# A linear-attention and state-space kernel whose program is ordered by one wanted time per unit of work, and whose last output leaves by four transfers

## The chip, the cores and the metric

The kernel runs on one core of one Trainium2 chip. The core has five engines that run side by side: TensorE (PE, matrix products, with its weight loads as PEld), VectorE (DVE), ScalarE (ACT), GpSimd (POOL) and SyncE (SP), which here issues every DMA. The metric is the device time of one execution in microseconds. Most executions of one kernel agree within 0.3%.

## The reference

Two independent layers read their own inputs, and their outputs stand side by side in the 1152 columns of each of the 2048 rows. The first is a state-space convolution (S4D), the second a linear attention whose feature map is a softmax and the softmax of the negated values, with 32 heads of 18 columns.

```python
def _A_ref(u, log_A_real, A_imag, C_real, C_imag, log_dt, D_skip):
    dt = jnp.exp(log_dt)
    A = -jnp.exp(log_A_real) + 1j * A_imag
    C = (C_real + 1j * C_imag) * dt[:, None]
    P = jnp.exp((A * dt[:, None])[:, :, None] * pos[None, None, :])
    K = 2.0 * jnp.einsum("dn,dnl->dl", C, P).real
...
    y = jnp.fft.irfft(Uf * Kf[None, :, :], L2)[:, :, :L]
...
    return y + u * D_skip[None, None, :]

def _B_ref(x, wqkv, w_phi, wo):
...
    pq = jnp.einsum("bhsd,hdf->bhsf", q, w_phi)
    pk = jnp.einsum("bhsd,hdf->bhsf", k, w_phi)
    phi_q = jnp.concatenate([_softmax(pq, axis=-1), _softmax(-pq, axis=-1)], axis=-1)
    phi_k = jnp.concatenate([_softmax(pk, axis=-1), _softmax(-pk, axis=-1)], axis=-1)
    kv = jnp.einsum("bhsf,bhsd->bhfd", phi_k, v)
    z  = jnp.einsum("bhsf->bhf", phi_k)
    num = jnp.einsum("bhqf,bhfd->bhqd", phi_q, kv)
    den = jnp.einsum("bhqf,bhf->bhq", phi_q, z)[..., None] + 1e-6
    return (num / den) ... @ wo
...
return jnp.concatenate([a, b], axis=-1)
```

L is 2048, D is 576, and the state has 128 entries for each of the 576 channels.

## The kernel before

The kernel's Python does not write its instructions in the order in which they run. It hands small pieces of work to a planner (class `Plan`): each call of `op` names an engine, an estimated cost, the tiles that it reads and writes, and a function that emits the instructions. `Plan.run` then walks through a made-up clock: at each step it looks, for each engine, at the pieces whose inputs are ready and whose tiles can be had, takes the best by a key, and emits it. The result is one fixed order of instructions for each engine's queue. The chip runs these queues; waits among them are real, and the planner's costs have no further effect. The key is

```python
key = (s if s > at[e] + 100.0 else at[e], ops[k][5], k)
```

Here `s` is the planned start of the piece and `at[e]` the time at which its engine is free. So among pieces that could start within 100 ns of the engine being free, the smaller wanted time (`ops[k][5]`) goes first. The wanted time also sets the order in which pieces take the slots of a tile with few buffers (`place` in `Plan.run`); "pa" and "pb", the PSUM tiles, are free of this order. The wanted time is `pl.now`, set ahead of each unit. Before the change, it grows evenly over the units of one kind:

```python
T_K, D_K = 21.6, 11.6
T_KV = 243.3
T_Q, D_Q = 259.8, 20.2
T_U, D_U = 4.5, 8.6
T_G, D_G = 39.9, 8.0
T_P, D_P, T_P2 = 188.6, 7.7, 393.5
T_Y, D_Y, T_Y2 = 335.1, 8.6, 586.1
```

The attention's units: `fold` multiplies the key weights and later the query weights by the feature map's matrices (tiles wah and wal, one buffer each, so the query weights overwrite the key weights once the last key tile has used them); `whole` loads the value and output weights (wbh, wbl). 16 key tiles (`key_tile`, 128 rows each) load x (tile xi, split into xh and xl), make four groups of 14 matmuls (`gemm`, L326 is the line of every matmul), a softmax (L439 to L449, with the tiles small and e) and a sum over all tiles in PSUM (kvt). `kv` turns that sum into the block matrix kvb. 16 query tiles (`query_tile`) make two such groups of matmuls, a softmax, eleven transposes (L519), the products with kvb, the division, five transposes of the result, two more groups of matmuls, and a store of 128 rows and 576 columns (tile ot, L561).

The convolution's units: 18 units of `u_first` transform the input and store it to DRAM (L587). `mags` and `sel_part` prepare magnitudes, `params` works out phases for 96 channels at a time (six blocks, `par`, for six groups each). 36 groups (`phases`, `waves`, `group`) make the filter for 16 channels each: GpSimd adds phases (PQ), ScalarE takes sines (cs) and exponentials (N), VectorE multiplies them (L747 to L752, into cs and E), and TensorE sums over the state (64 small matmuls reading E and cs). After every ninth group, `k_first` transforms a quarter of the filter and stores it (L772). 2 x 16 `product` units load a block of the input's and the filter's spectrum and of the matrices (ub, kb, cm; L812 to L814), multiply (VectorE L337, then GpSimd), transform back and store (zo, L852). The first half needs two quarters of the filter (groups 0 to 17), the second half the other two. 2 x 8 `last` units load zi (L863, two loads each; the first load needs all 16 products of its half), make 32 matmuls, copy the two PSUM tiles to yo, by VectorE and ScalarE, and store yo by two transfers of 128 partitions (L877). The tile yo has two buffers, zi two, e three, PSUM four of each kind.

`first` is shared by `u_first` and `k_first`: two matmuls, on the upper and lower 64 rows, were two entries of the plan, the second ordered behind the first.

Of the kernel before, what the change touches and what calls it, by code (L numbers as in the profile page):

```python
# [22 lines left out]
W = 4 * DG  # L23
# [108 lines left out]
class Plan:  # L132
# [9 lines left out]
    def __init__(self):  # L142
        self.ops, self.pools, self.free, self.window, self.strict = [], {}, {}, {}, {}
        self.now = 0.0
# [8 lines left out]
    def op(self, eng, cost, fn, r=(), w=(), with_=(), early=0.0, table=None, busy=1.0, lock=False):  # L153
        deps = set()
        for b in r:
            deps.update(b.writers)
        for b in w:
            deps.update(b.readers)
        k = len(self.ops)
        for b in r:  # L160
            b.readers.append(k)
        for b in w:
            b.writers.append(k)
        bufs = list({id(b): b for b in (*r, *w, *with_) if not isinstance(b, Mark)}.values())
        for b in bufs:
            b.left += 1
        self.ops.append([eng, cost, fn, deps, bufs, self.now - early, table, busy, lock and eng])
# [129 lines left out]
PAIR = False  # L297
T_K, D_K = 21.6, 11.6
T_KV = 243.3
T_Q, D_Q = 259.8, 20.2  # L300
T_U, D_U = 4.5, 8.6
T_G, D_G = 39.9, 8.0
T_P, D_P, T_P2 = 188.6, 7.7, 393.5
T_Y, D_Y, T_Y2 = 335.1, 8.6, 586.1


def body(tc, nc, i, out, ctx):
# [27 lines left out]
    def tt(eng, dst, a, b, alu, r, w, n):  # L335
        e = dve if eng == "dve" else pool
        op(eng, c_dve(n) if eng == "dve" else c_pool(n), lambda: e.tensor_tensor(dst(), a(), b(), op=alu), r=r, w=w,  # L337
           lock=eng == "pool" or n > 99 and not any(x.tag in ("pa", "pb") for x in r))
# [8 lines left out]

    ident, ii = B("ident", [128, 128]), B("xl", [128, 128], I32)
# [10 lines left out]
    def fold(w_t):  # L359

        hi, lo, phiw = B("wah", [128, 5, D], F32R), B("wal", [128, 5, D], F32R), B("fT", [128, 5, 126])
        op("sp", 1000, lambda: sp.dma_start(phiw.t, i["wphi"]), w=[phiw])

        def block(g, c, cs):
            wt, pa, pb = B("e", [128, D]), B("pb", [128, 4, 126]), B("pb", [128, 126])
            op("sp", c_dma(c * D * 4), lambda: sp.dma_start(wt.t[:c], w_t[cs, :]), w=[wt])

            def f():
                for k in range(4):
                    mm(pa.t[:, k, :c], wt.t[:c, k * 128:k * 128 + 128], phiw.t[:c, g, :c])  # L370
# [5 lines left out]
            op("pe", 2 * 215, f, r=[wt, phiw], w=[pb], with_=[hi, lo])  # L376
# [33 lines left out]
    def gemm(x, w, ps, o, cs):  # L410

        (xh, xl), (wh, wl) = x, w

        def f():
            p = o()
            for k in range(4):
                mm(p, xh.t[:, k, :], wh.t[:, k, cs], k == 0, False)
                mm(p, xh.t[:, k, :], wl.t[:, k, cs], False, False)
                mm(p, xl.t[:, k, :], wh.t[:, k, cs], False, False)
            mm(p, xh.t[:, 4, :], wh.t[:, 4, cs], False, False)  # L420
            mm(p, xh.t[0:64, 4, :], wl.t[0:64, 4, cs], False, True)
        op("pe", 14 * max(109, (cs.stop - cs.start) / 2.4 + 15), f, r=[xh, xl, wh, wl], w=[ps], busy=0.93)
# [33 lines left out]
    pl.now = 0.0  # L456
    wk = fold(i["wkT"])
    wv = whole(i["wv"])
    kvt = B("pb", [128, 8, 36])
# [27 lines left out]
    pl.now = T_KV  # L487
# [15 lines left out]

    wq = fold(i["wqT"])
    wo = whole(i["wo"])

    def query_tile(t):
        pl.now = T_Q + D_Q * t
# [60 lines left out]
    pl.now = T_U  # L569
# [20 lines left out]
    for c in range(18):  # L590
        pl.now = T_U + D_U * c
# [3 lines left out]
    pl.now = 0.0  # L595
# [7 lines left out]
    def mags():  # L603
# [9 lines left out]
        op("dve", c_dve(n), lambda: dve.scalar_tensor_tensor(C.t, C.t, 1e-30, I.t, op0=ALU.add, op1=ALU.add), r=[C, I], w=[C])  # L613
        op("act", c_act(n), lambda: act.activation(C.t, C.t, AF.Ln), r=[C], w=[C], table="ln")
        op("dve", c_dve(n), lambda: dve.scalar_tensor_tensor(C.t, C.t, 0.5, bc(ldc), op0=ALU.mult, op1=ALU.add), r=[C, ldc], w=[C])
# [11 lines left out]
    pl.now = T_G - 30  # L627
    mags()
    pl.now = 0.0
# [6 lines left out]
    for k in range(3):  # L636
        sel_part(k)
# [6 lines left out]
    def params(blk):  # L644
# [15 lines left out]
        def vs(x, s0, o0, dst, s1=None, o1=None, z=None):  # L660
            k = {} if o1 is None else dict(op1=o1)
            op("dve", c_dve(BW, True), lambda: dve.tensor_scalar(z() if z else dst.t, x.t, s0, s1, op0=o0, **k), r=[x], w=[dst])
# [17 lines left out]
        def flip(full, dst, z=None):  # L680
# [13 lines left out]
        op("dve", c_dve(4 * BW, True), lambda: dve.tensor_scalar(fx.t, p4(), MAGIC, MAGIC, op0=ALU.add, op1=ALU.subtract), r=[pi], w=[fx])  # L694
        tt("dve", p4, p4, lambda: fx.t, ALU.subtract, [pi, fx], [pi], 4 * BW)
        op("dve", c_dve(4 * BW, True), lambda: dve.tensor_scalar(p4().bitcast(I32), p4(), TWO32, BELOW, op0=ALU.mult, op1=ALU.min),
           r=[pi], w=[pi])
# [6 lines left out]
    def phases(g, par):  # L704
        pl.now = T_G + D_G * g
# [7 lines left out]
            x()[:, :, :, 0], pi.t[:, 0:3:2, gs].bitcast(I32).rearrange("p r d -> p d r")), r=[pi], w=[PQ])  # L713
# [8 lines left out]
    def waves(PQ, also):  # L722
# [7 lines left out]
        op("act", 3 * c_act(65 * W) + 250, f, r=[PQ, hp, *also], w=[cs], table="sin")  # L730
        return cs

    def group(g, par, cs, ks):
        pl.now = T_G + D_G * g
# [26 lines left out]
        op("pe", 970, f, r=[E, cs], w=[ps], with_=[ks], busy=0.57)  # L761
# [17 lines left out]
    pl.now = T_G + 20  # L779
# [5 lines left out]
    for g in range(0, NG, 2):  # L785
        blk = g // (NG // NB)
        if par[blk] is None:
            pl.now = T_G + D_G * g - 6
            par[blk] = params(blk), exponents(blk)
        pq = [phases(h, par[blk]) for h in (g, g + 1)]  # L790
        for j, h in enumerate((g, g + 1)):
            pl.now = T_G + D_G * g
# [3 lines left out]
            group(h, par[blk], waves(pq[j], pq[1:] if PAIR and j == 0 else ()), ks)  # L796
            if (h + 1) % (NG // NQ) == 0:
                pl.now = T_G + D_G * h
# [7 lines left out]
    def product(p, half):  # L806

        pl.now = (T_P, T_P2)[half] + D_P * p
# [50 lines left out]
    def last(cb, half):  # L859
        pl.now = (T_Y, T_Y2)[half] + D_Y * cb / 4  # L860
# [11 lines left out]
        op("pe", 520, f, r=[zi, w3], w=ps, with_=[yo], busy=0.4)  # L872
        for r in range(2):
            copy("act" if r else "dve", lambda r=r: yo.t[:, r], lambda r=r: ps[r].t, [ps[r]], [yo], HD)
        for r in range(2):
            st = out.ap[0][0]
            op("sp", c_dma(64 * 2304, 1152), lambda r=r: sp.dma_start(bass.AP(  # L877
                tensor=out.tensor, offset=out.offset + (32 * r + cb) * st + HD * half, ap=[[st, 4], [64 * st, 32], [1, HD]]),
                yo.t[:, r]), r=[yo])
# [26 lines left out]
```

## Time and profile before

| what | before |
|---|---|
| median of 3 runs | 754.59 us |
| lowest, highest | 754.41, 755.47 us |
| the profiled execution's own time | 755.61 us |
| its span, first to last instruction | 753.8 us |
| mean granted TensorE clock | 0.939 |
| bytes moved by DMA | 102.29 MB |

The span is what the trace covers; the time includes what lies around it, 1.8 us here. The clock is a share of full speed. Below, a stage is a stretch of the span between two times, and a row of it gives each engine's busy time in that stretch. The chain of waits is the chain of work that ended last, followed back from the last instruction to what released it.

The 40 slices of the page show the five engines over the span (each digit is the busy share in tenths):

```profile
PE   6799998997997888867999989999979999999965
DVE  2678899877779889687877577786544555555531
ACT  3748787586686877677878576997423335333321
POOL 0475355665555858556857345772103233243100
```

### The profile page before, as it was taken

What the parts mean: (1) busy time and instruction counts of PE and PEld (TensorE: products, weight loads), DVE (VectorE), ACT (ScalarE), POOL (GpSimd) and SP (SyncE); (2) the same over time, 40 slices, a digit from 0 to 9 for tenths busy, and PEclk for the clock granted to TensorE, in tenths of its full rate; (3) what the DMA queues carried; (4) which work ended last, traced back from release to release, by engine and by line L of the source; (5) the groups of instructions that cost most, each with busy time, mean ns of one, the idle gap of its engine ahead of it and who ended that gap; (6) DMA issues with size and microseconds to landing.
All of it is one profiled execution on the core that took longest, in us unless ns stands there. A gap on an engine that the chain in (4) does not pass through costs nothing.

```text
span 753.8 us, 18023 instructions
## 1 busy us (share of the span) xinstructions
PE 670.2 (89%) x7188; PEld 496.6 (66%) x7188; DVE 520.7 (69%) x961; ACT 465.0 (62%) x823; POOL 350.9 (47%) x471
## 2 busy tenths in 40 slices
PE   6799998997997888867999989999979999999965
PEld 4577786874776675645766757766757676768753
DVE  2678899877779889687877577786544555555531
ACT  3748787586686877677878576997423335333321
POOL 0475355665555858556857345772103233243100
PEclk9899999997999987878999999999989999999996
DMA  8943435135441112532455643434577746562653
GB/s 228 334 123 90 129 77 173 53 103 138 103 110 38 50 51 77 122 80 75 139 154 156 175 140 126 156 115 121 133 197 210 234 148 182 154 196 95 180 157 106
DMA packets 114791, 102.29 MB, mean 136 GB/s; under 512 B 43604, under 2 KB 96724, under 8 KB 114708
## 3 DMA queue, kind: packets, MB, share of 16 engines
q1 hardware_dynamic: 114708, 101.15, 47.4%
q8 instruction: 57, 0.93, 0.5%
q14 instruction: 26, 0.21, 0.1%
HBM read 61.98 MB, written 39.06 MB: 134 GB/s over the span
## 4 chain that ended last, share of the span: by engine, by line
PE 47%; DVE 24%; DMA 10%; ACT 8%; issue 2%; POOL 1%; SPq 0%; ACTq 0%; DVEq 0%; POOLq 0%
PE pb L326 26%; PE pa L326 18%; DMA zi<-dram 4%; DVE e L337 4%; DMA out_dram<-yo 3%; DVE small L448 2%; DVE E L748 2%; DVE E L752 2%; DVE E L750 2%; DVE cs L747 2%; DVE ac L337 1%; PE pb L519 1%; DMA dram<-yo 1%; DMA kb<-dram 1%; ACT cs L729 1%
## 5 line engine op out<-in xcount | busy, mean ns | idle before, releaser
L716 POOL TENSOR_TENSOR PQ<-PQ,pi 128x32 int32<-128x32 int32 (+4 forms) x180 | 140.9, 796 | 4.7
L326 PE MATMUL pb<-wah,xh 128*128 128x288 f32 (+2 forms) x320 | 105.9, 331 | 5.1 <-DVE wal L337 3.0
L326 PE MATMUL pb<-wal,xh 128*128 128x288 f32 (+4 forms) x320 | 105.9, 331 | 0.0
L337 POOL TENSOR_TENSOR e<-small,e 128x576 f32<-128x576 f32 x32 | 42.4, 1324 | 126.2 <-DVE small L337 122.7
L337 POOL TENSOR_TENSOR ac<-ac 128x288 f32<-128x288 f32 x64 | 53.6, 853 | 66.8 <-DVE ac L337 64.2
L326 PE MATMUL pb<-wah,xl 128*128 128x288 f32 (+2 forms) x256 | 79.9, 312 | 0.8 <-POOL xl L337 0.8
L326 PEld LDWEIGHTS pb<-wah,xh 128*128 128x128 f32 x320 | 64.5, 202 | 23.8 <-issue 11.6
L326 PE MATMUL pb<-wbh,xl 128*128 128x288 f32 (+2 forms) x256 | 76.8, 300 | 0.5 <-DVE xl L337 0.5
L337 POOL TENSOR_TENSOR xl<-xi,xh 128x512 fp32r<-128x512 f32 x32 | 46.1, 1440 | 65.1 <-ACT xh L331 58.0
L326 PEld LDWEIGHTS pb<-wal,xh 128*128 128x128 f32 (+1 forms) x320 | 64.0, 200 | 11.0 <-issue 9.3
L439 DVE TENSOR_REDUCE small<-pb 128x16 f32<-128x288 f32 (+2 forms) x64 | 28.7, 449 | 57.6 <-PE pb L326 56.3
L448 DVE TENSOR_REDUCE small<-e 128x64 f32<-128x1152 f32 x32 | 43.1, 1345 | 34.7 <-ACT e L447 34.7
L337 DVE TENSOR_TENSOR ac<-us,pa 128x288 f32<-128x288 f32 x128 | 49.8, 444 | 23.7 <-PE pa L326 20.1
L741 ACT ACTIVATE N<-pa 128x512 f32<-128x512 f32 x108 | 60.3, 602 | 5.3 <-PE pa L326 2.7
L326 PE MATMUL pa<-E,cs 128*32 128x64 f32 x2304 | 44.2, 231 | 12.3 <-DVE E L750 5.3
L747 DVE TENSOR_TENSOR cs<-N,cs 128x1024 f32<-128x1024 f32 x36 | 47.4, 1317 | 8.6 <-ACT cs L729 8.4
L326 PEld LDWEIGHTS pa<-E,cs 128*32 128x32 f32 x2304 | 37.2, 116 | 24.5 <-issue 4.3
L326 PEld LDWEIGHTS pb<-wah,xl 128*128 128x128 f32 x256 | 51.9, 203 | 1.1 <-POOL xl L337 1.1
L326 PE MATMUL pb<-wbh,xi 128*128 128x288 f32 x160 | 51.6, 323 | 0.7 <-ACT xi L331 0.7
L326 PE MATMUL pb<-wbh,xh 128*128 128x270 f32 (+1 forms) x160 | 51.3, 321 | 1.0 <-DVE e L337 1.0
L326 PE MATMUL pb<-wbl,xi 128*128 128x288 f32 (+1 forms) x160 | 51.4, 321 | 0.0
L326 PE MATMUL pb<-wbl,xh 128*128 128x270 f32 (+3 forms) x160 | 51.0, 319 | 0.0
(126 smaller groups left out, 1657.0 us busy)
## 6 DMA issues: line engine op xcount, KB each, us to landing
xi<-in_xT_dram SPq DMA_DIRECT2D x32, 320.0 KB
dram<-zi SPq DMA_DIRECT2D x36, 256.0 KB
dram<-yo SPq DMA_DIRECT2D x64, 144.0 KB
ub<-dram SPq DMA_DIRECT2D x32, 288.0 KB
kb<-dram SPq DMA_DIRECT2D x32, 288.0 KB
dram<-zo SPq DMA_DIRECT2D x32, 288.0 KB
zi<-dram SPq DMA_DIRECT2D x32, 288.0 KB
cm<-in_mats_dram SPq DMA_DIRECT2D x32, 256.0 KB
```

The lines of the kernel that those rows point to most:

```text
L326: pe.matmul(o, l, r, start=start, stop=stop, skip_group_check=skip)
L337: op(eng, c_dve(n) if eng == "dve" else c_pool(n), lambda: e.tensor_tensor(dst(), a(), b(), op=alu), r=r, w=w, lock=eng == "pool" or n > 9 ...
L439: op("dve", c_dve(DH * m), lambda: dve.tensor_reduce(mx.t, v(), axis=AX.X, op=ALU.max), r=[p], w=[mx])
L448: op("dve", 1270, lambda: dve.tensor_reduce(sm.t, e.t, axis=AX.X, op=ALU.add), r=[e], w=[sm])
L519: pe.transpose(tp.t[0:36 * m, k, :], head(e, 3 * (g0 + k), m), ident.t)
L716: op("pool", c_pool(2 * n * W), lambda n=n, j=j: pool.tensor_tensor(x()[:, :, :, n:2 * n], x()[:, :, :, 0:n], pi.t[:, j:j + 2, gs].bitcast ...
L729: act.activation(cs.t[:, 0], cs.t[:, 0], AF.Sin, scale=-TURN, bias=hp.t)
L741: op("act", c_act(512), lambda: act.activation(dst.t.rearrange("p x y -> p (x y)"), ps.t, AF.Exp), r=[ps], w=[dst], table="exp")
L747: op("dve", c_dve(64 * W), lambda: dve.tensor_tensor(F(), both(M.t), F(), op=ALU.mult), r=[M, cs], w=[cs], lock=True)
L748: op("dve", c_dve(64 * W), lambda: dve.tensor_tensor(E.t[:, :, :, 32:64], both(up.t), cs.t[:, :, :, 0:32], op=ALU.mult), r=[up, cs], w=[E] ...
L750: op("dve", c_dve(32 * W), lambda: dve.tensor_tensor(E.t[:, 0, :, 0:32], dn.t, cs.t[:, 0, :, 32:0:-1], op=ALU.mult), r=[dn, cs], w=[E], lo ...
L752: op("dve", c_dve(32 * W), lambda: dve.scalar_tensor_tensor(E.t[:, 1, :, 0:32], dn.t, -1.0, cs.t[:, 1, :, 32:0:-1], op0=ALU.mult, op1=ALU. ...
```

## The change

The wanted times come from a table. `Plan.at(name, k)` looks up the time for unit k of a kind, and each of the tiles, groups, blocks and products has its own value, in place of a start and a step. The values are on another scale than before, and some are negative; only their order counts for the key above. Beside that:

- Some of the planner's costs are changed: products of `fold` (860 to 1070 and 430 to 530), `gemm` (35 more), `group` (970 to 1035), `last` (520 to 850, with a higher share counted as busy), `first` (one entry of 2.08 n + 40 in place of two of 1.03 n).
- More of VectorE's and GpSimd's pieces carry the planner's lock, which keeps locked pieces of these two engines from being planned at the same time.
- `first` plans its two matmuls as one entry.
- A `last` unit stores yo by four transfers of 32 partitions, each with both halves of the tile, in place of two of 128 partitions with one half each.
- `PAIR`, which was False, is gone.

No unit of work is added or left out.

```diff
+    def at(self, name, k=0):
+        self.now, self.unit = WANT[name][k], (name, k)
...
+WANT = dict(
+    ident=[200],
+    start=[1798.2],
+
+    key=[-314.4, -292.7, -260.8, -73, 103.2, 70.3, 69.8, 43.7, 76.5, 95.3, 128.2, -58.1, 135.6, 192.9, 160, 89.8],
+
+    kv=[-544.3],
+
+    fold=[-1066, -537.7, 291.1, 337.1],
+
+    query=[345.9, 782.5, 1116.5, 526.7, 291.8, 505.4, 786.8, 530.6, 653.5, 543.6, 1034.6, 1210.9, 716.3, 909.9,
+          1249.5, 1259.8],
+
+    u=[-548.6, -447.9, 0.1, -619, -510.9, -220.5, -1113.5, -323.6, -72, -247.3, -476, -73.2, -420.6, -359.5, -64,
+          -141.3, -91.9, 130],
+
+    mags=[-744.2],
+    sel=[-932.4, -431.1, -659.5],
+
+    par=[-1086.9, -18.5, 292.3, 308.4, 337.3, 379.1],
+
+    group=[-150.2, -78.2, -143.1, -425, -192.9, -79.4, 70, -6.9, -123.6, 116.5, 76.5, 141, 135.1, 120.5, 199.9,
+          148.8, 138.9, 121.7, 222.9, 223.5, 236.7, 270.4, 387, 307.8, 374.4, 310.6, 337.7, 458.7, 527.1, 469.4,
+          449.1, 486, 945.8, 1067.3, 618.7, 1033.5],
+    dsk=[-1082.1],
+
+    kfirst=[-227, -209.6, -69.8, 664],
+    product=[286.4, 210.6, 136.9, 250.1, 228.6, 472.9, 518.4, 357, 135.7, 423.4, 205.6, 461.2, 433.7, 325.7, 461.2,
+          324.2, 815.9, 625.5, 644.5, 864.3, 588.8, 676.2, 694.2, 1003.3, 789.4, 775.5, 536.7, 777.7, 1072.7, 801.3,
+          882.2, 965],
+    last=[962.5, 1303, 1293.8, 1087.1, 1040.5, 998.8, 830.7, 743.1, 1540, 2123.9, 1373.8, 1493.8, 2152.1, 1555.8,
+          1410.9, 1315.2],
+)
...
     def tt(eng, dst, a, b, alu, r, w, n):
...
-           lock=eng == "pool" or n > 99 and not any(x.tag in ("pa", "pb") for x in r))
+           lock=eng == "pool" or not any(x.tag in ("pa", "pb") for x in r))
...
-            op("pe", 4 * 215, f, r=[wt, phiw], w=[pa], with_=[hi, lo])
+            op("pe", 1070, f, r=[wt, phiw], w=[pa], with_=[hi, lo])
...
-        op("pe", 14 * max(109, (cs.stop - cs.start) / 2.4 + 15), f, r=[xh, xl, wh, wl], w=[ps], busy=0.93)
+        op("pe", 14 * max(109, (cs.stop - cs.start) / 2.4 + 17.5), f, r=[xh, xl, wh, wl], w=[ps], busy=0.93)
...
-    pl.now = 0.0
+    pl.at("fold", 0)
     wk = fold(i["wkT"])
+    pl.at("fold", 1)
     wv = whole(i["wv"])
...
     def key_tile(t):
-        pl.now = T_K + D_K * t
+        pl.at("key", t)
...
     def first(b, src, n, o, dst, view):
         ps = [B("pa", [128, n]) for _ in range(2)]
-        for h in range(2):
-            hs = slice(64 * h, 64 * h + 64)
-            op("pe", n * 1.03, lambda h=h, hs=hs: mm(ps[h].t, w1.t[hs, :], src(hs)), r=[w1, b, *ps[:h]], w=[ps[h]], with_=ps)
+
+        def f():
+            for h in range(2):
+                hs = slice(64 * h, 64 * h + 64)
+                mm(ps[h].t, w1.t[hs, :], src(hs))
+        op("pe", 2.08 * n + 40, f, r=[w1, b], w=ps)
...
         if par[blk] is None:
-            pl.now = T_G + D_G * g - 6
+            pl.at("par", blk)
...
             if (h + 1) % (NG // NQ) == 0:
-                pl.now = T_G + D_G * h
+                pl.at("kfirst", qt)
...
     def last(cb, half):
-        pl.now = (T_Y, T_Y2)[half] + D_Y * cb / 4
+        pl.at("last", 8 * half + cb // 4)
...
-        op("pe", 520, f, r=[zi, w3], w=ps, with_=[yo], busy=0.4)
+        op("pe", 850, f, r=[zi, w3], w=ps, with_=[yo], busy=0.6)
...
-        for r in range(2):
+        for n in range(4):
             st = out.ap[0][0]
-            op("sp", c_dma(64 * 2304, 1152), lambda r=r: sp.dma_start(bass.AP(
-                tensor=out.tensor, offset=out.offset + (32 * r + cb) * st + HD * half, ap=[[st, 4], [64 * st, 32], [1, HD]]),
-                yo.t[:, r]), r=[yo])
+            op("sp", c_dma(32 * 2304, 1152), lambda n=n: sp.dma_start(bass.AP(
+                tensor=out.tensor, offset=out.offset + (n + cb) * st + HD * half, ap=[[64 * st, 32], [32 * st, 2], [1, HD]]),
+                yo.t[32 * n:32 * n + 32]), r=[yo])
```

More of the change, by code (lines that the diff above doesn't have):

```diff
@@ L143, in __init__ @@
         self.ops, self.pools, self.free, self.window, self.strict = [], {}, {}, {}, {}
-        self.now = 0.0
+        self.now, self.unit = 0.0, None
     def tag(self, name, pool, n, window=None):
@@ L166, in op @@
             b.left += 1
-        self.ops.append([eng, cost, fn, deps, bufs, self.now - early, table, busy, lock and eng])
+        self.ops.append([eng, cost, fn, deps, bufs, self.now - early, table, busy, lock and eng, (self.unit, early)])
     def emit(self, k, o):
@@ L345, in body @@
     halves = (slice(0, 288), slice(288, 576))
+    pl.at("ident")
     ident, ii = B("ident", [128, 128]), B("xl", [128, 128], I32)
@@ L375, in f @@
                     mm(pb.t[r:r + 64, :c], wt.t[:c, 512:576], phiw.t[:c, g, :c])
-            op("pe", 2 * 215, f, r=[wt, phiw], w=[pb], with_=[hi, lo])
+            op("pe", 530, f, r=[wt, phiw], w=[pb], with_=[hi, lo])
             a, b = (lambda x: x.t[:, 0:4, cs]), (lambda x: x.t[:, 4, cs])
@@ L454, in body @@
     head = lambda b, h0, n: b.t.rearrange("p h s f -> p h (s f)")[:, h0:h0 + n, :]
-    pl.now = 0.0
+    pl.at("fold", 0)
     wk = fold(i["wkT"])
+    pl.at("fold", 1)
     wv = whole(i["wv"])
+    pl.at("start")
     kvt = B("pb", [128, 8, 36])
@@ L485, in body @@
         key_tile(t)
-    pl.now = T_KV
+    pl.at("kv")
     kvs, kvh, kvb = B("o", [128, 8, 36]), B("ot", [36, H + 1, 19]), B("kvb", [108, 11, 3, 19])
@@ L502, in body @@
             kvb.t[36 * r:36 * r + 36, 0:n, r, :], kvh.t.rearrange("p (g r) f -> p g r f", r=3)[:, 0:n, r, :]), r=[kvh], w=[kvb])
+    pl.at("fold", 2)
     wq = fold(i["wqT"])
+    pl.at("fold", 3)
     wo = whole(i["wo"])
     def query_tile(t):
-        pl.now = T_Q + D_Q * t
+        pl.at("query", t)
         ps = gemm_halves(load_x(t), wq)
@@ L568, in body @@
     kd, zd = ([B("dram", [64, 64, HD]) for _ in range(2)] for _ in range(2))
-    pl.now = T_U
+    pl.at("u", 0)
     op("sp", 600, lambda: sp.dma_start(w1.t, i["w1"]), w=[w1])
@@ L590, in body @@
     for c in range(18):
-        pl.now = T_U + D_U * c
+        pl.at("u", c)
         u_first(slice(512 * c, 512 * c + 512))
-    pl.now = 0.0
+    pl.at("mags")
     sel, ld, ldc = B("sel", [4 * W, 96 * W], F32R), B("ld", [128, 5]), B("ldc", [128, 5])
@@ L625, in mags @@
             keep(l, 2 * j + 1)
-    pl.now = T_G - 30
     mags()
-    pl.now = 0.0
     def sel_part(k):
@@ L636, in body @@
     for k in range(3):
+        pl.at("sel", k)
         sel_part(k)
@@ L661, in vs @@
             k = {} if o1 is None else dict(op1=o1)
-            op("dve", c_dve(BW, True), lambda: dve.tensor_scalar(z() if z else dst.t, x.t, s0, s1, op0=o0, **k), r=[x], w=[dst])
+            op("dve", c_dve(BW, True), lambda: dve.tensor_scalar(z() if z else dst.t, x.t, s0, s1, op0=o0, **k), r=[x], w=[dst], lock=True)
         a(AF.Exp, dt, dt)
@@ L693, in params @@
         ip = lambda k, n=1: pi.t[:, k:k + n].bitcast(I32)
-        op("dve", c_dve(4 * BW, True), lambda: dve.tensor_scalar(fx.t, p4(), MAGIC, MAGIC, op0=ALU.add, op1=ALU.subtract), r=[pi], w=[fx])
+        op("dve", c_dve(4 * BW, True), lambda: dve.tensor_scalar(fx.t, p4(), MAGIC, MAGIC, op0=ALU.add, op1=ALU.subtract), r=[pi], w=[fx], lock=True)
         tt("dve", p4, p4, lambda: fx.t, ALU.subtract, [pi, fx], [pi], 4 * BW)
         op("dve", c_dve(4 * BW, True), lambda: dve.tensor_scalar(p4().bitcast(I32), p4(), TWO32, BELOW, op0=ALU.mult, op1=ALU.min),
-           r=[pi], w=[pi])
+           r=[pi], w=[pi], lock=True)
         tt("pool", lambda: ip(2), lambda: ip(2), lambda: ip(3), ALU.add, [pi], [pi], BW)
@@ L704, in phases @@
     def phases(g, par):
-        pl.now = T_G + D_G * g
+        pl.at("group", g)
         pi = par[0]
@@ L712, in phases @@
         op("pool", 260, lambda: pool.tensor_copy(
-            x()[:, :, :, 0], pi.t[:, 0:3:2, gs].bitcast(I32).rearrange("p r d -> p d r")), r=[pi], w=[PQ])
+            x()[:, :, :, 0], pi.t[:, 0:3:2, gs].bitcast(I32).rearrange("p r d -> p d r")), r=[pi], w=[PQ], lock=True)
         for k in range(5):
@@ L720, in phases, with waves @@
         return PQ
-    def waves(PQ, also):
+    def waves(PQ):
         cs = B("cs", [128, 2, W, 65])
@@ L729, in f @@
             act.activation(cs.t[:, 0], cs.t[:, 0], AF.Sin, scale=-TURN, bias=hp.t)
-        op("act", 3 * c_act(65 * W) + 250, f, r=[PQ, hp, *also], w=[cs], table="sin")
+        op("act", 3 * c_act(65 * W) + 250, f, r=[PQ, hp], w=[cs], table="sin")
         return cs
     def group(g, par, cs, ks):
-        pl.now = T_G + D_G * g
+        pl.at("group", g)
         mg = par[1]
@@ L760, in f @@
                         mm(ps.t[32 * m:32 * m + 32, d, :], cs.t[:, r, c * DG + d, 33:65], E.t[:, r, c * DG + d, :], r == 0, r == 1, True)
-        op("pe", 970, f, r=[E, cs], w=[ps], with_=[ks], busy=0.57)
+        op("pe", 1035, f, r=[E, cs], w=[ps], with_=[ks], busy=0.57)
         d0 = g % (NG // NQ) * DG
@@ L778, in body @@
     dsk = B("dsk", [128, NQ, DQ])
-    pl.now = T_G + 20
+    pl.at("dsk")
     op("dve", 200, lambda: dve.memset(dsk.t, 0.0), w=[dsk])
@@ L791, in body @@
         for j, h in enumerate((g, g + 1)):
-            pl.now = T_G + D_G * g
+            pl.at("group", h)
             qt, first_of = divmod(h, NG // NQ)
@@ L795, in body @@
                 ks = B("ks", [128, 64, DQ])
-            group(h, par[blk], waves(pq[j], pq[1:] if PAIR and j == 0 else ()), ks)
+            group(h, par[blk], waves(pq[j]), ks)
             if (h + 1) % (NG // NQ) == 0:
-                pl.now = T_G + D_G * h
+                pl.at("kfirst", qt)
                 tt("dve", lambda ks=ks: ks.t[:, 0, :], lambda ks=ks: ks.t[:, 0, :], lambda qt=qt: dsk.t[:, qt], ALU.add,
@@ L806, in product @@
     def product(p, half):
-        pl.now = (T_P, T_P2)[half] + D_P * p
+        pl.at("product", 16 * half + p)
         blk = lambda b: b.t.rearrange("(p j r) b d -> p (r b) j d", j=2, r=2)[p]
```

12 lines of the change are left out of this document (2 added, 10 removed).

## The prediction

> **What bounds the kernel now.** The page's first two lines come first: TensorE is busy for 670.2 of 753.8 us, and no other engine comes near that.
>
> ```profile
> span 753.8 us, 18023 instructions
> PE 670.2 (89%) x7188; PEld 496.6 (66%) x7188; DVE 520.7 (69%) x961; ACT 465.0 (62%) x823; POOL 350.9 (47%) x471
> ```
>
> An average over unlike stages says little, so the span is cut where the work changes. The rows that mark the cuts are those of single tiles (the first and last start is the last pair of numbers before the semicolon).
>
> ```profile
> L326 PE MATMUL pb<-wbh,xh x160: 282/303/592, 39.6 to 275.7; 128*128 128x270 f32 x80, 128*128 128x306 f32 x80
> L326 PE MATMUL pa<-E,cs x2304: 216/219/318, 76.6 to 519.9; 128*32 128x64 f32 x192
> L519 PE MATMUL pb<-ident,e x176: 272/273/459, 323.9 to 727.4; 128*108 128x128 f32 x160, 128*72 128x128 f32 x16
> ```
>
> Key tiles end at 276, the 36 groups of the state-space filter run from 77 to 520, and queries reach their transposes from 324 on. The stages, one row each (start:end, length, busy us of each engine with its instructions, granted TensorE clock, DMA share, GB/s):
>
> ```profile
> 0.00:60.00 60.00, 49.17 (x247) 36.90 (x247) 33.83 (x75) 33.19 (x57) 25.16 (x40) 0.94 0.76 227
> 60.00:280.00 220.00, 200.94 (x2951) 156.51 (x2950) 187.67 (x316) 163.86 (x258) 127.69 (x189) 0.94 0.34 91
> 280.00:360.00 80.00, 60.40 (x650) 42.80 (x649) 64.68 (x106) 61.53 (x98) 50.05 (x70) 0.79 0.36 89
> 360.00:520.00 160.00, 151.08 (x1779) 107.67 (x1777) 120.63 (x204) 125.80 (x223) 93.96 (x115) 0.99 0.50 147
> 520.00:720.00 200.00, 187.99 (x1417) 138.67 (x1406) 105.69 (x248) 73.76 (x174) 54.03 (x59) 0.98 0.59 167
> 720.00:753.80 33.80, 20.60 (x165) 14.01 (x163) 8.21 (x16) 6.90 (x16) 0.00 (x0) 0.81 0.47 140
> ```
>
> TensorE loses time in two ways: it stands idle (length less busy), or it works at a lowered clock (busy times one less the clock). By stage, idle plus slow clock: 10.8 + 3.0, 19.1 + 12.1, 19.6 + 12.7, 8.9 + 1.5, 12.0 + 3.8, 13.2 + 3.9, together 83.6 + 36.9 = 120.5 us. A change that only reorders lives on these 120.5 us: the work at full clock, 753.8 - 120.5 = 633 us, stays. The loss is dense where groups share VectorE with keys (60 to 280, VectorE 85% busy), where keys hand over to queries (280 to 360), and at the end. Between 360 and 520 there is little to fetch.
>
> What holds the end up is in the chain of waits (start, us, what):
>
> ```profile
> 564.47 9.53 DMA out_dram<-yo
> 574.06 10.05 DMA out_dram<-yo
> 584.13 8.12 DMA zi<-dram
> 694.59 2.21 DMA dram<-zo
> 696.94 3.47 DMA zi<-dram
> 709.51 8.31 DMA zi<-dram
> 728.51 9.06 DMA zi<-dram
> ```
>
> The reader sees one kind of load, zi, take 3.47 us in one place and 8 to 9 us where stores of yo stand among the loads.
>
> **The change part by part.** *The four stores.* Two stores of 128 partitions become four of 32 for each of 16 steps. What a store of the old form costs, from the timeline near the end, then its issues, then its size and that of zo (sizes from the DMA view of 520 to 754):
>
> ```profile
> 720.47 1.28 SPq L877 DMA_DIRECT2D out_dram<-yo  x2
> 726.73 0.46 DVE L333 COPY yo<-pa 128x288 f32<-128x288 f32 x1 [0.62 <-DMA out_dram<-yo]
> 747.45 1.18 SPq L877 DMA_DIRECT2D out_dram<-yo  x2
> ...
> L877 SPq DMA_DIRECT2D out_dram<-yo x32: 537/577/1827, 545.3 to 748.1; - x32
> L561 SPq DMA_DIRECT2D out_dram<-ot x16: 335/351/2113, 361.1 to 746.7; - x16
> ...
> out_dram<-yo SPq DMA_DIRECT2D x32, 144.0 KB
> dram<-zo SPq DMA_DIRECT2D x16, 288.0 KB
> ```
>
> The stores issued by 721.75 free yo only at 726.7, 5 us later, while zo with twice the bytes lands in 2.21 us. So the old store is slow for its size, and the span's own end shows it again: issues done at 748.63, end at 753.8, 5.2 us. In code, the old store's DRAM side has 4 as its outermost length, the new one has 32, as its SBUF side has. I take the new store to land like zo, in 2.2 us. Four issues cost between 4 x 0.351 and 4 x 0.577 us (the two rows above; half the elements in each pulls toward the lower), so the last ends 0.2 to 1.1 us later than now. Landing saves 3.0 us less that: about 2 us at the very end. The zi loads of the last half stand behind such stores; two of them, at 8.31 and 9.06 instead of 3.47, lose 4.8 and 5.6 us, part of it covered by query products. I take 3 us. Tail together: 5 us, between -1.1 (new stores land as slowly as old ones and only the issues are added) and 13.
>
> The Trainium skill, DMA: Bandwidth & Descriptors, "Why a DMA increments its semaphore by 16 and not by 1", says that the outermost length of each side sets how many DMA engines a transfer uses, at most 16 and a divisor of both: by that the old store runs on 4 engines and the new one on 16, which agrees with 5 us against 2.21 us, though no row here counts engines. The same page's "Rules for kernel authors" speaks against splitting: two transfers to disjoint partition halves serialize, so one of 128 partitions is advised. By that rule alone the landing saves nothing, the tail term is -1 in place of +5, and the sum would be 726.
>
> The other 32 new issues (64 stores in place of 32) take at most 32 x 0.577 = 18.5 us of SP's queue. SP waits far longer than that:
>
> ```profile
> SPq L812 <- PE pa L326: 74.9, 24, 12.6
> ```
>
> This one line of SP's waits is 74.9 us, so I cost them at nothing; behind them stand zi, xi and cm loads, and without that cover each step would push its neighbours back by 0.2 to 1.1 us, 3 to 18 us over 16 steps.
>
> *Costs and locks of the planner* (products, groups, folds, last step; locks between VectorE and GpSimd) emit no instruction. Nor does joining the two products of `first` into one entry: the same two matmuls, now always neighbours. These act only through the order.
>
> *The table.* It removes and adds no instruction, but re-ranks all. I read it by sorting. Three things differ from the evenly spaced times of before. First, the parameters of groups 12 to 17 (`par` 2) rank 292, behind every key tile (the last is 193) and beside the first query and the wq fold; before, they ranked 130 among keys up to 196. Of the groups whose products ran in 60 to 280, groups 0 to 11 stay with the keys. How many ran there, and the group's VectorE work, from all instructions that touch N (VectorE and ScalarE us):
>
> ```profile
> L326 PE MATMUL pa<-E,cs x1088: 216/219/246, 76.6 to 278.5; 128*32 128x64 f32 x182
> ...
> 60.00:280.00 220.00, 72.54 (x68) 30.86 (x55) 0.94 0.34 91
> ```
>
> At 64 products each, 1088 are 17 groups, and 72.54 / 17 = 4.3 us of VectorE a group. Five fewer take 21 us off a VectorE busy for 188 of 220 us, and land where it is busy 75% or 53% (the rows of 360 and 520). Second, with groups 12 on beside queries, the hand-over has work of both kinds. Third, only queries 2, 11, 14 and 15 rank behind the last group (33, at 1067); before, ten left after 520.
>
> What this is worth cannot be read off one row, so each stage is bounded by nothing (a new stall as long as the old one) and by its whole loss above. I take: 0 to 60, 2 of 13.8 (the DMA share there is 0.76, and all of what is first needed must still come in); 60 to 280, 12 of 31.2, a good third, about half of the 21 us VectorE gives up; 280 to 360, 15 of 32.3, half; 360 to 520, none; 520 to 720, 4 of 15.8, the spread stores among it. A fixed order meets delays it was not made for, so I take back 3 for new stalls. Sum: 2 + 12 + 15 + 0 + 4 + 5 - 3 = 35 us. The profiled execution took 755.61 us with 1.8 us around its span of 753.8; 755.61 - 35 = 720.6, and the median of the three runs is 754.59, 1.0 lower: **720 us** rounded.
>
> A check from the other side: ten queries after 520 become four. One query's TensorE work is four gemms, two of which take 4.50 us back to back, plus transposes and small products:
>
> ```profile
> 630.21 4.50 PE pb L326 x28
> ...
> L326 PE MATMUL pb<-kvb,fT 108*128 108x57 f32 (+1 forms) x352 | 44.8, 279 | 1.6 <-ACT fT L331 1.6
> L519 PE MATMUL pb<-ident,e 128*108 128x128 f32 (+1 forms) x176 | 25.1, 282 | 10.9 <-DVE e L337 10.2 <-ACT fT L331 0.5
> ```
>
> 9.0 + 44.8/16 + 25.1/16 = 13.4 us; six are 80 us. So the last group moves from 520 to 520 - 29 + 80 = 571, and 719 - 571 = 148 us are left for what hangs on it: the second half's products and last steps. They move bytes (DMA view and slices of 520 to 754, 5.85 us each):
>
> ```profile
> GB/s 67 105 103 181 175 145 247 187 210 217 209 208 231 254 108 208 111 160 131 241 241 151 196 121 241 207 131 154 101 1 181 186 186 109 141 199 188 133 94 59
> DMA packets 35748, 38.13 MB, mean 163 GB/s; under 512 B 10256, under 2 KB 30736, under 8 KB 35728
> zi<-dram SPq DMA_DIRECT2D x28, 288.0 KB
> out_dram<-ot SPq DMA_DIRECT2D x10, 288.0 KB
> xi<-in_xT_dram SPq DMA_DIRECT2D x8, 320.0 KB
> ```
>
> Six queries less take off 6 x 608 KB = 3.7 MB. Twelve of the 28 zi loads and half of the 32 yo stores are the first half's (5.9 MB); five of its eight steps now rank ahead of group 33, another 3.7 MB. That leaves 30.7 MB in 148 us: 207 GB/s, below the 220 that the eight slices from 247 to 254 average. The forecast fits, without much room.
>
> **The rivals.** *The transfers become the bound after the last group* (slower). Place: from the end of group 35 to the end. Price: 30.7 MB at the 163 GB/s of before is 188 us, 571 + 188 = 759, 760 us as a median. It decides below 30.7 MB / (753.8 - 571) = 168 GB/s. For it: before moves 163 there on average. Against: then TensorE was 94% busy and asked for no more (DMA share 0.59), and the eight slices held 220.
>
> *VectorE keeps its grip* (small gain): groups moved off the keys meet queries instead, whose softmax is VectorE's too, and the two middle gains shrink from 27 to 6 with the rest as it was: 741 us. For it: VectorE is 81% busy in 280 to 360 already.
>
> *The table fills nearly everything*: two thirds of each middle loss (21 + 22), 5 at the start, 3 in 360 to 520, 10 in 520 to 720, 9 at the end, less 3: 67 us, 688 us. Against: 89% busy becomes 97%, and each group, softmax and product is a chain over three or four engines.
>
> *The order changes nothing that counts*: TensorE-bound stages remain, gains and new stalls cancel: 754.6. Against it speaks the tail term, which needs no table.
>
> **How the numbers follow.** Forecast (703 to 738) 0.53; VectorE 0.17 (738 to 753); fills nearly everything 0.11 (683 to 703); no change 0.04; transfers 0.15 (756 to 782). About 0.2%, 1.5 us, is what a measurement of this kernel can tell from no change. Faster is 0.53 + 0.17 + 0.11 = 0.81, same 0.04, slower 0.15. The range 696 to 757 leaves out about 0.07 below and 0.13 above. The forecast's own range is 703 to 738.
>
> **What would show it.** Stores of yo that release their tile in about 2 us, 64 issues of 0.35 to 0.58 us, and an end 3 us or less after the last issue: the tail. VectorE under 85% while keys run and a clock near 0.95 between keys and queries: the middle. The last group's matmul near 571 and four or five stores of ot after it: the shift. Wrong would be zi or kb loads of 8 us and more on the chain after the last group with TensorE under 85% (transfers), or VectorE over 90% across the hand-over (the VectorE rival).

## The result, and the profile after

| what | before | after |
|---|---|---|
| median | 755.03 us (4 runs) | 721.39 us (4 runs, 720.15 to 729.51) |
| ratio | 1 | 0.956, 95% interval 0.9491 to 0.9629 |
| run again (11 and 6 runs) | 758.27 us | 721.63 us, ratio 0.9525 (0.9488 to 0.9562) |

The change makes the kernel faster by some 34 us; the forecast was 720 us, inside a range of 696 to 757. Executions spread wider here than the 0.3% named at the start and the 0.2% of the prediction: the eleven of the kernel before in the last row lie between 754.58 and 763.94 us, and a ratio is known to 0.4 to 0.7%. The page of the first profiled execution:

```profile
span 727.7 us, 18071 instructions
PE 667.3 (92%) x7188; PEld 496.6 (68%) x7188; DVE 509.9 (70%) x961; ACT 468.9 (64%) x828; POOL 341.5 (47%) x471
```

That execution was the slowest of its four (729.51 us), so a second profile of the same kernel, taken in a later run with a span of 722.1 us, is read from here on. Its rows by stage (start:end, length, busy us of PE, PEld, DVE, ACT and POOL, granted clock, DMA share, GB/s), cut at 280 and at the last group:

```profile
0.00:60.00 60.00, 43.94 (x213) 32.83 (x213) 33.76 (x88) 38.42 (x62) 34.32 (x57) 0.94 0.76 223
60.00:280.00 220.00, 210.68 (x3186) 166.90 (x3185) 190.54 (x314) 174.17 (x276) 120.24 (x180) 0.94 0.38 97
280.00:511.00 231.00, 207.74 (x2227) 146.78 (x2227) 172.81 (x296) 176.84 (x302) 138.88 (x177) 0.90 0.47 127
511.00:722.10 211.10, 199.72 (x1568) 147.99 (x1568) 113.03 (x265) 79.66 (x190) 50.28 (x57) 0.99 0.65 181
```

The kernel before, with its last two stages cut at its last group:

```profile
280.00:520.00 240.00, 211.48 (x2427) 150.46 (x2425) 185.31 (x309) 187.33 (x320) 144.01 (x185) 0.92 0.45 127
520.00:753.80 233.80, 208.59 (x1580) 152.68 (x1568) 113.89 (x264) 80.66 (x190) 54.03 (x59) 0.96 0.57 163
```

TensorE's loss (length less busy times clock) by stage, before and after: 13.8 and 18.7, 31.1 and 22.0, 45.4 and 44.0, 33.6 and 13.4 us. The start is worse by 4.9, the key stage better by 9.1, the hand-over and what follows better by 1.4, and the stage behind the last group better by 20.2. That is 25.8 of the 31.7 us between the spans; the other 5.9 are in the product of busy time and clock, which should not change, and which the clock's two digits leave open by some 3 us in each kernel.

The rows that mark the stages after, with the same columns as in the prediction (last key gemm, groups, first transposes of a query, stores of ot behind the last group):

```profile
L356 PE MATMUL pb<-wbh,xh x160: 282/299/593, 42.6 to 245.8; 128*128 128x270 f32 x80, 128*128 128x306 f32 x80
L356 PE MATMUL pa<-E,cs x2304: 216/219/318, 69.0 to 510.7; 128*32 128x64 f32 x192
L554 PEld LDWEIGHTS pb<-ident,e x176: 114/131/216, 308.2 to 701.6; 128*108 128x108 f32 x160, 128*72 128x72 f32 x16
...
L361 ACT ACTIVATE ot<-pb x20: 392/411/439, 526.2 to 713.3; 128x288 f32<-128x288 f32 x20
```

The key tiles end at 246 in place of 276. Of these 30 us, 16 are left at the first transposes (308 for 324) and 9 at the last group (511 for 520). Behind that group stand twenty copies into ot, that is ten queries, just as many as before. The chain of waits behind the last group has three waits for a DMA of over 2 us left, and none for a store to the output:

```profile
515.12 4.33 DMA dram<-yo
520.29 2.62 DMA dram<-yo
689.57 4.79 DMA zi<-dram
```

### The profile page after: what moved, and what is told of

It is laid out like the page before. It is cut to its first block, busy times and chain, and to the rows that moved or that the text cites. A ratio compares the mean times of both kernels' runs of the same rounds, so it can differ in the third digit from the quotient of the medians.

```text
span 727.7 us, 18071 instructions
## 1 busy us (share of the span) xinstructions
PE 667.3 (92%) x7188; PEld 496.6 (68%) x7188; DVE 509.9 (70%) x961; ACT 468.9 (64%) x828; POOL 341.5 (47%) x471
## 4 chain that ended last, share of the span: by engine, by line
PE 67%; ACT 12%; DVE 11%; DMA 4%; issue 2%; SPq 1%; POOL 1%; DVEq 0%; ACTq 0%; POOLq 0%
PE pb L356 39%; PE pa L356 24%; PE pb L554 3%; DVE E L789 2%; ACT cs L766 2%; DMA e<-in_wkT_dram 2%; ACT cs L764 1%; ACT N L778 1%; DVE E L785 1%; DVE E L787 1%; PE pb L584 1%; ACT L765 1%; DMA dram<-yo 1%; DVE cs L784 1%; ACT cs L765 1%
## 5 line engine op out<-in xcount | busy, mean ns | idle before, releaser
L753 POOL TENSOR_TENSOR PQ<-PQ,pi 128x512 int32<-128x512 int32 (+4 forms) x180 | 129.5, 725 | 8.0
L356 PE MATMUL pb<-wah,xh 128*128 128x288 f32 (+2 forms) x320 | 101.9, 319 | 0.0
L356 PE MATMUL pb<-wal,xh 128*128 128x288 f32 (+4 forms) x320 | 101.9, 318 | 0.0
L356 PE MATMUL pb<-wah,xl 128*128 128x288 f32 (+2 forms) x256 | 76.6, 299 | 0.0
L356 PEld LDWEIGHTS pb<-wah,xh 128*128 128x128 f32 x320 | 61.1, 191 | 15.9 <-issue 12.9
L367 DVE TENSOR_TENSOR ac<-us,pa 128x288 f32<-128x288 f32 x128 | 49.8, 447 | 30.8 <-PE pa L356 20.2
L356 PEld LDWEIGHTS pb<-wal,xh 128*128 128x128 f32 (+1 forms) x320 | 60.8, 190 | 10.5 <-issue 8.4
L784 DVE TENSOR_TENSOR cs<-N,cs 128x1024 f32<-128x1024 f32 x36 | 49.2, 1368 | 24.1 <-ACT cs L766 22.5
L367 POOL TENSOR_TENSOR xl<-xi,xh 128x512 fp32r<-128x512 f32 x32 | 44.8, 1400 | 45.4 <-ACT xh L361 37.6
L356 PE MATMUL pa<-E,cs 128*32 128x64 f32 x2304 | 49.0, 241 | 18.0 <-DVE E L787 9.7
L356 PEld LDWEIGHTS pa<-E,cs 128*32 128x32 f32 x2304 | 40.4, 123 | 33.0 <-DVE E L789 8.0
L356 PE MATMUL pa<-sel,mg 64*128 64x512 f32 x108 | 53.9, 538 | 4.2 <-ACT yo L618 1.1
```

The costliest lines, as they stand in the source:

```text
L356: pe.matmul(o, l, r, start=start, stop=stop, skip_group_check=skip)
L753: op("pool", c_pool(2 * n * W), lambda n=n, j=j: pool.tensor_tensor(x()[:, :, :, n:2 * n], x()[:, :, :, 0:n], pi.t[:, j:j + 2, gs].bitcast ...
L784: op("dve", c_dve(64 * W), lambda: dve.tensor_tensor(F(), both(M.t), F(), op=ALU.mult), r=[M, cs], w=[cs], lock=True)
```

## The experiments

Twelve kernels ran; each ratio is to the kernel before, run beside it on the same chip. Two theories stood against each other: the prediction's (the table fills TensorE in the middle, the stores are worth little) and its reverse (the stores carry what was gained behind the last group).

**The four stores alone, in the order of before.**

```diff
-            op("sp", ..., lambda r=r: sp.dma_start(bass.AP(... ap=[[st, 4], [64 * st, 32], [1, HD]]), yo.t[:, r]), r=[yo])
+            def store(r=r):
+                for n in (2 * r, 2 * r + 1):
+                    sp.dma_start(bass.AP(... ap=[[64 * st, 32], [32 * st, 2], [1, HD]]), yo.t[32 * n:32 * n + 32])
+            op("sp", ..., store, r=[yo])
```

> The kernel before, its order of instructions kept, with the four stores of 32 partitions in place of the two of 128 in each last step. By the prediction's sum the stores are worth 5 us at the end and at most the 4 us of 520 to 720: 746 to 750 us. Rival (the stores carry most of what was gained behind the last group, 20 us in the trace of the change): 735 to 740 us. Rival (splitting only adds issues): 755 to 757 us. The zi loads at 8 to 9 us on the chain should fall to 3 to 4 us by the first two.

Measured: 745.31 us, 0.9849 (0.9808 to 0.989), 11 us faster. That is just under the prediction's range and 5 us above the rival's. Pieces of its chain, and its two last stages:

```profile
558.20 3.98 DMA zi<-dram
694.80 3.46 DMA zi<-dram
727.30 4.68 DMA zi<-dram
...
280.00:520.00 240.00, 214.09 (x2419) 152.15 (x2417) 186.84 (x307) 186.90 (x321) 144.27 (x184) 0.90 0.47 127
520.00:745.70 225.70, 209.70 (x1568) 153.83 (x1568) 113.83 (x264) 80.67 (x190) 54.43 (x59) 0.95 0.62 169
```

The waits of 8 to 10 us for zi and out_dram are gone from the chain: zi takes 3.5 to 4.7 us. Between the two profiled executions, the whole gain lies behind the last group (226 us in place of 234), where the stores are.

**The table with the old two stores, in the order of the change.** Two of the four entries emit the old transfers, the others nothing.

> The changed kernel, its order kept, with the old two stores of 128 partitions. By the prediction's sum 6 to 9 us slower than the change: 727 to 730 us. Rival (the stores carry most): 736 to 741 us. Rival (the order alone, the stores do nothing): 721 us.

Measured: 732.15 us, 0.9667 (0.9627 to 0.9706). The order alone is worth 3.3%, some 25 us; the stores bring 10.5 us in this order too (732.15 to 721.63, medians beside different runs of before; 1.4% by the ratios). The effects multiply: 0.9849 x 0.9667 = 0.952, against 0.9525 for both.

**Everything but the table.**

```diff
+_T = dict(..., key=[21.6 + 11.6 * t for t in range(16)], query=[259.8 + 20.2 * t for t in range(16)], ...)
+WANT = _T
```

> Everything of the change (costs, locks, four stores) but the wanted times of before in place of the table. By the prediction's sum the table brings 27 us in the middle and 2 at the start, so some 748 to 752 us. Rival (the truer costs and locks reorder enough by themselves): 735 us or less. If the stores carry most, about the time of the stores alone.

Measured: 773.68 us, 1.0212 (1.0179 to 1.0244): slower than the kernel before, and 28 us slower than the same wanted times and the same stores with the old costs. None of the expectations held. The changed costs, the locks and the joined entry, with the even times, make the order worse; which of the three does it was not tried.

**The table smoothed.**

```diff
+    elif _n in ("key", "query", "u", "group", "par", "kfirst"):
+        WANT[_n] = _even(_v)   # the fitted line through the sorted values
```

`product` and `last` are smoothed half by half. The values are sorted first, so the units of a kind also go back into the order of their numbers.

> The changed kernel with the table's times smoothed: each kind of unit keeps its level, but its units are evenly spaced along a fitted line, in their own order, held within the kind's first and last time. If only the levels and the spread of the kinds count, 718 to 727 us. If each unit's own time counts, 735 us or more.

Measured: 766.32 us, 1.0126 (1.008 to 1.0172). Levels and spread of the kinds alone don't bring the gain; each unit's own time counts, be it by its distance to others or by its rank within its kind, which this kernel does not tell apart.

**The change once more.**

> The changed kernel once more, for a profile nearer to its median (the first profiled execution took 729.51 us, the median was 721.39). All theories: 720 to 724 us. If the ten queries behind the last group and the last group near 514 us are the order's and not that execution's, they show again: ten stores of ot after it. If the prediction's shift holds at all, the last group would be near 571 us with four.

Measured: 721.63 us; its profile is the one above. Ten queries behind the last group, last group at 511: the prediction's shift is not there.

**The table with the old costs and locks.** All the changed costs and locks are set back, and `first` has its two entries again.

> The changed kernel with the table and the four stores, but the planner's costs and locks of before, and the two entries of first. If the table's times are worth what they are on their own (levels and ranks), 721 to 730 us. Rival (table and costs are one fit, and the table is worth nothing with other costs): 745 us or more, as the old times with the new costs were 773.

Measured: 777.15 us, 1.027 (1.0222 to 1.0319). The rival's side: table and costs belong together.

**Two stores of 128 rows in the order of before.**

```diff
-                tensor=out.tensor, offset=out.offset + (32 * r + cb) * st + HD * half, ap=[[st, 4], [64 * st, 32], [1, HD]]),
+                tensor=out.tensor, offset=out.offset + (64 * cb + 128 * r) * st % (2048 * st) + HD * half, ap=[[st, 128], [1, HD]]),
```

> The kernel before, its order kept, with two stores of 128 partitions whose DRAM side is 128 rows in a row (outermost length 128 in place of 4); the convolution's rows of the output land in other rows than the reference's, bytes and runs of 1152 as before. If the outermost length of 4 made the old stores slow, 742 to 747 us, as with the four stores alone, or a little less for half the issues. Rival (the tile's split into 32 partitions did it): 755 us, and yo still freed 5 us after the issue.

Measured: 736.98 us, 0.9718 (0.9675 to 0.976), better than the four stores. So it was not the split: two stores of 128 partitions are no slower once their DRAM side does not begin with a length of 4. (Here the 128 rows also lie side by side. The four stores keep the rows where they were, and gain too; the outermost length is what both have changed.) From the last issue to the end of the span are 2.4 us (733.7 + 0.4 to 736.5), as with the four. Their issues are cheap as well (ns, least/median/most):

```profile
L877 SPq DMA_DIRECT2D out_dram<-yo x32: 332/383/577, 546.5 to 733.7; - x32
```

against 577 ns for the old store, and in the change:

```profile
L914 SPq DMA_DIRECT2D out_dram<-yo x64: 570/593/1304, 540.9 to 719.0; - x64
```

**One value moved: the first fold ahead of all.**

```diff
-    fold=[-1066, -537.7, 291.1, 337.1],
+    fold=[-2000, -537.7, 291.1, 337.1],
```

> The changed kernel with the first fold ranked ahead of all (-2000 in place of -1066), which puts the loads of the key weights ahead of u 6, the first parameters and dsk. The change's trace shows TensorE waiting 9.8 us for them in the first 20 us, and 5.9 us less busy in the first 60 us than before. If that start is lost time, 714 to 719 us. If the later stages absorb it, 721. If the fitted order is broken by any move, 725 us or more.

Measured: 776.42 us, 1.0238 (1.0193 to 1.0282). One value of some 150 takes away all of the gain and more. Its groups, its start and the stages around its last group:

```profile
L356 PE MATMUL pa<-E,cs x2304: 216/219/318, 62.0 to 557.1; 128*32 128x64 f32 x192
...
0.00:60.00 60.00, 43.68 (x277) 32.03 (x277) 36.87 (x80) 40.21 (x67) 31.65 (x53) 0.83 0.82 243
60.00:280.00 220.00, 202.42 (x3019) 162.06 (x3019) 179.81 (x303) 171.22 (x260) 116.74 (x178) 0.94 0.34 90
280.00:558.00 278.00, 242.90 (x2491) 174.87 (x2491) 193.82 (x350) 190.31 (x332) 142.08 (x189) 0.88 0.41 112
558.00:773.50 215.50, 185.20 (x1406) 129.50 (x1405) 99.68 (x229) 71.90 (x173) 50.35 (x54) 0.91 0.63 171
```

The groups begin 7 us earlier than in the change and end 46 us later; the start itself loses 23.7 us, where the change loses 18.7. The last row shows what the prediction had hoped a shift would do: one query less is left (nine stores of ot, 1406 matmuls for 1568), and yet the stage is 4 us longer than the change's, with TensorE idle for 30 us at a clock of 0.91.

**Two of the four stores from ScalarE's queue, in the order of before and in that of the change.**

Shown against the four stores alone:

```diff
-                    sp.dma_start(bass.AP(
+                    (act if n > 1 else sp).dma_start(bass.AP(
```

> The kernel before, its order kept, four stores of 32 partitions, two of each four issued by ScalarE's queue in place of SP's. Four stores on SP gave 0.985 of before, two stores of 128 rows 0.972. If that difference is the 593 ns that each of 64 issues holds SP's queue, with zi and kb loads behind it, halving SP's share brings 0.975 to 0.98. If the smaller stores themselves move slower, 0.985 as before. If ScalarE's work is now held up by the issues, 0.99 or more.

Measured: 743.70 us, 0.9815 (0.9779 to 0.985), against 0.9849 from SP alone. The intervals overlap, so how much of the 1.3% between four stores and two of 128 rows is SP's queue stays open.

> The changed kernel, its order kept, with two of each four stores issued by ScalarE's queue. If SP's issues are late work behind the last group, 714 to 719 us, and the last issue ends 2.4 us earlier after the last copies. If TensorE is the bound there (it is busy 200.7 of 212 us behind the last group), the end alone, 719 to 720 us. If ScalarE's queue is held up, 723 us or more.

Measured: 720.91 us, 0.9513 (0.9477 to 0.9549). It is no different from the change within the interval, which fits a TensorE that is busy for 200 of the 211 us behind the last group.

**Two stores of 128 rows in the order of the change.** The edit is that of the same stores above; two of the four entries are empty.

> The changed kernel, its order kept, with two stores of 128 rows in a row in place of the four (the convolution's rows land in other rows than the reference's). If the stores' issues cost what they do in the order of before (1.3% between the two forms), 711 to 714 us. If the fitted order has room for them, 718 to 721 us.

Measured: 717.43 us, 0.9465 (0.9429 to 0.95), some 4 us better than the change (721.63); the intervals overlap a little (0.9488 to 0.95). Its rows land elsewhere, so it is a bound for cheaper stores and not a version to keep.

**One value moved: the parameters of groups 12 to 17.**

```diff
-    par=[-1086.9, -18.5, 292.3, 308.4, 337.3, 379.1],
+    par=[-1086.9, -18.5, 60.0, 308.4, 337.3, 379.1],
```

> The changed kernel with one value of the table moved, the parameters of groups 12 to 17 (60 in place of 292), ahead of most key tiles instead of behind them. By the prediction's reading this takes VectorE work back among the keys: 727 to 740 us, with VectorE busier and fewer key tiles done by 280. If the order is a fit that any moved value undoes, 740 to 778 us, as one moved fold gave 776. If this value does not matter, 721 us.

Measured: 763.12 us, 1.0053 (1.0022 to 1.0084). Its groups, its last key gemm, its groups up to 252, and its key stage:

```profile
L356 PE MATMUL pa<-E,cs x2304: 216/219/318, 68.6 to 533.7; 128*32 128x64 f32 x192
L356 PE MATMUL pb<-wbh,xh x160: 282/300/597, 42.2 to 251.8; 128*128 128x270 f32 x80, 128*128 128x306 f32 x80
L356 PE MATMUL pa<-E,cs x896: 218/219/316, 68.6 to 244.0; 128*32 128x64 f32 x180
...
60.00:280.00 220.00, 206.96 (x3100) 164.20 (x3098) 180.65 (x300) 166.23 (x264) 112.58 (x173) 0.92 0.39 99
```

VectorE is less busy there than in the change (180.7 for 190.5 us), where my reading of the value said busier, and the key tiles end at 252, 6 us later than in the change and long before 280. One rank moved makes the kernel 42 us slower, and not by way of the VectorE work that the value was read for.

## Why the prediction was right, and where it was not

The sum was right (35 us expected, 34 found). The split between order and stores was nearly so: 5 to 9 us expected of the stores and the rest of the order, 11 and 25 found. The places were not, and so the sum is in good part luck: the start was to bring 2 us and lost 4.9, the two middle terms were to bring 27 and brought 10.5, and behind the last group 9 were expected and 20 found.

- *What bounds the kernel.* TensorE's loss as the stock that a reordering lives on held: the two gains come out of its idle time and its slow clock, and TensorE goes from 89% to 92% busy.
- *60 to 280: 12 us expected, 9 found* between these two times. But the keys end 30 us earlier in the change, so equal times hold unequal work. Cut at the last key, the first transposes and the last group instead, the change and then the kernel before:

```profile
60.00:246.00 186.00, 182.83 (x2705) 146.46 (x2703) 159.15 (x259) 144.45 (x229) 96.81 (x150) 0.97 0.40 102
246.00:308.00 62.00, 47.84 (x686) 35.45 (x685) 57.95 (x96) 51.88 (x84) 41.98 (x53) 0.75 0.45 105
308.00:511.00 203.00, 187.75 (x2022) 131.76 (x2022) 146.26 (x256) 154.69 (x266) 120.33 (x155) 0.92 0.44 124
...
60.00:276.00 216.00, 196.94 (x2868) 153.40 (x2866) 185.59 (x310) 160.63 (x250) 124.09 (x184) 0.94 0.34 91
276.00:324.00 48.00, 36.55 (x424) 26.82 (x424) 38.63 (x69) 36.24 (x61) 31.72 (x38) 0.82 0.41 98
324.00:520.00 196.00, 178.93 (x2086) 126.76 (x2085) 148.76 (x248) 154.32 (x267) 115.90 (x151) 0.95 0.46 133
```

While keys run, TensorE loses 8.7 us in place of 30.9, 22 less, which is more than forecast. The reason given does not hold, though. Groups 0 to 11 were to stay with the keys and 12 to 17 to move out, with VectorE under 85%. Fourteen groups run there in place of sixteen (the rows below, 64 products a group: the change up to 246, before up to 276), the order that the planner emits has 12, 13 and 17 among them, and VectorE is 86% busy in both (159.15 of 186, 185.59 of 216).

```profile
L356 PE MATMUL pa<-E,cs x896: 216/219/314, 69.0 to 240.6; 128*32 128x64 f32 x180
...
L326 PE MATMUL pa<-E,cs x1024: 216/219/246, 76.6 to 272.9; 128*32 128x64 f32 x171
```

- *280 to 360: 15 us expected, 1 found* from 280 to the last group. At the prediction's own cut the loss of 280 to 360 falls from 32.3 to 26.0 us (80.00 - 66.63 x 0.81), and that of 360 to the last group grows from 10.4 to 18.4 (151.00 - 141.11 x 0.94), where no change was forecast. Cut by the work, the hand-over is worse than before: by the rows above, TensorE loses 26.1 us between the last key and the first transposes (18.0 before), and 30.3 from there to the last group (26.0 before). So 12 of the 22 us won with the keys are lost again. The granted clock between keys and queries is 0.75, where near 0.95 was to show that the middle came true.
- *The shift of the last group from 520 to 571: false.* This is the step that failed outright, and it is a misreading of the code, not of the trace. A wanted time orders the pieces that take turns in one small tile, and otherwise only ranks those that could start within 100 ns of a free engine. Groups and queries share no such tile. So only queries 2, 11, 14 and 15 rank behind group 33, but that does not put the other twelve before it: ten queries remain behind it, as before. The check by 30.7 MB in 148 us rested on this shift and proves nothing; 38.13 MB went out in some 211 us, and the rival of the transfers never came into play.
- *Behind the last group: 9 us expected, 20 found.* The size was off twice. The stores: 5 to 9 us expected, 11 found by the medians, 8 between the two profiled executions. They gain where the prediction looked, among the last steps. Here are the rows behind 695, of the kernel before and of the four stores alone:

```profile
695.00:753.80 58.80, 42.34 (x348) 31.78 (x346) 21.96 (x50) 13.64 (x31) 4.08 (x4) 0.89 0.52 147
...
695.00:745.70 50.70, 40.17 (x330) 29.54 (x328) 20.27 (x45) 13.77 (x31) 4.09 (x4) 0.88 0.66 165
```

TensorE's loss in these rows is 21.1 and 15.4 us, so some 6 of the 7 us by which the loss of the whole stage fell lie here. The steps of the first half, whose waits of 8 to 10 us are gone from the chain too, brought little. The rest is the order: with the same stores, the change needs 211 us behind its last group and the order of before 226. TensorE's loss there is 13.4 and 26.5 us (225.70 - 209.70 x 0.95), 11.4 and 16.0 of it idle and the rest, 2.0 and 10.5, slow clock. By these figures more than half of what the order gains here is clock. In the order of before, with the four stores, these two pieces lose most:

```profile
520.00:545.00 25.00, 23.26 (x129) 17.47 (x130) 10.43 (x21) 8.70 (x23) 2.91 (x3) 0.86 0.42 96
...
720.00:745.70 25.70, 16.55 (x129) 10.86 (x114) 6.54 (x15) 5.00 (x13) 0.00 (x0) 0.76 0.57 150
```

- *The new store.* Its landing was right: from the last issue (719.0 + 0.6) to the end of the span are 2.5 us in the change, 5.2 before. Its issue was not: I took half the elements to pull the cost toward 351 ns, and it is 593 ns, more than the old 577. The Trainium skill, DMA: Bandwidth & Descriptors, "Why a DMA increments its semaphore by 16 and not by 1", ties the number of DMA engines to the outermost lengths; that agrees with the two stores of 128 rows, which gain as much as the four and more, though no row here counts engines. The advice against splitting in the same page's "Rules for kernel authors" agrees as well: the split is a price (0.9849 against 0.9718), paid for an outermost length of 32.
- *SP's queue cost nothing: open.* The two stores of 128 rows, whose issues are cheaper, gave 1.3% over the four in the old order and 0.6% in the new, but other things in them differ too; half of the issues on another queue gave nothing that can be told apart. SP's issues do stand on the chain at the end of the old order, in front of the last load of zi and 28 matmuls that take 6.18 us where the same took 4.50 us elsewhere (four stores alone):

```profile
726.01 0.59 SPq L880
726.70 0.55 SPq L863
727.30 4.68 DMA zi<-dram
732.02 1.21 PE pa L326 x14
733.23 6.18 PE pb L326 x28
```

- *0 to 60, 2 us expected, and new stalls, 3 us:* the start loses 4.9 us more. The loads of the key weights no longer lead, but with them put first the stage lost 23.7 us in place of 18.7 and the kernel 55, so that is not shown as the cause.
- *The reasons read off the table* (a late `par`, a rank behind keys) are not shown to explain any of the gain: two groups fewer stand with the keys, but the kernel with the one `par` moved has fourteen there as well (896 products up to 252) and is 42 us slower. Five kernels that changed part of table or costs, two of them one value, gave 763 to 777 us. That the table is the pick among many orders, valid only with its costs and as a whole, fits all five; how it was found no run can show. Which waits a moved value turns over, piece by piece, was not traced, so why this order is better stays open below the level of stages.

## What to carry to other kernels

Look at the outermost length on the DRAM side of a store that lands slowly: here four stores with 32 in place of two with 4 saved 11 us of 756, and two with 128 there saved more still. A list of wanted times steers a greedy planner, and does not say when things run: read the gain from the trace, by stages cut at the same work and not at the same time, and don't explain single values before one has been moved and timed. Where one moved value of 150 costs more than the table gains, table, costs and locks are one object, to be fitted again after any edit.

## What the runs showed of the hardware that was not expected

The time that SP's queue needs to issue a store does not follow its bytes or elements: 577 ns for 128 partitions with a DRAM side of 4 x 32 runs, 383 ns for the same 144 KB in 128 rows (422 in the order of the change), 593 ns for half of it as 32 partitions of two runs each. From ScalarE's queue, the last form took 582 ns in the order of the change:

```profile
L914 ACTq DMA_DIRECT2D out_dram<-yo x32: 577/582/1802, 539.6 to 717.1; - x32
```
